# Projection of a filter-and-bilinear kernel: the third weight as the stationary operand, 512 tokens as the moving one

## The chip, the core and the metric

The kernel runs on one core of a Trainium2 chip. The metric is the device time of one execution in microseconds (us). The kernel before takes 2495.35 us, the median of three runs (2493.35 to 2497.64). Matmuls run on TensorE (PE in the profile; the load of a stationary operand is PEld), elementwise work on VectorE (DVE), ScalarE (ACT) and GpSimd (POOL); DMAs are issued from the SyncE (SP) and ScalarE queues.

## The reference

```
x: (8, 3072, 256)   filt_r, filt_i: (1537, 256)   w_a, w_b: (256, 1536)   w_out: (1536, 256)

X = np.fft.rfft(x, axis=1)
y = np.fft.irfft(X * (filt_r + 1j * filt_i)[None], n=3072, axis=1)   # a filter along the sequence
t = y.reshape(8 * 3072, 256)
out = ((t @ w_a) * (t @ w_b)) @ w_out                                # (24576, 256), fp32
```

The change touches only the last product, `(a * b) @ w_out`, and the order in which its result is stored.

## The kernel before, in words

**Tiling.** The transform along the sequence is made as matrix products of length 24 and 128 (the lines `s1`, `s2`, `is1`, `is2`, each on one pair of columns, row groups or token groups at a time). The rest works on visits `(b, c, p)`: batch `b` of 8, column group `c` of 6 (512 tokens each), slice `p` of 6 (256 of the 1536 hidden features). That is 288 visits. For a visit, seven products (`product`, the bilinear step with fewer multiplications) go to the PSUM banks x, y and z, ACT and DVE add them up to `c0` and `c1`, DVE multiplies their halves (`parts`, L678) to two gated tiles `g` of 128 features by 512 tokens each, called f0 and f1.

**Two halves of a number.** TensorE's fast fp32r form keeps fewer bits than fp32. So each operand is split in a high and a low half: `split` makes `gh` on ACT (L686) and then `gl = g - gh` on POOL (L687), and the third weight lies in SBUF as `wo_h` and `wo_l` for good. A product is three matmuls: high by high, low weight by high, high weight by low.

**The projection.** `project(r, f)` (L691) adds one gated tile, times its 128 rows of `w_out`, to the column group's result. That stands in two PSUM banks `po0` and `po1` over the 12 projections of a column group (6 slices by f0 and f1), 576 projections in all. Before, a block of 128 tokens of `gh` or `gl` is the stationary operand and the 256 columns of the weight move: 4 blocks by 3 terms is 12 matmuls of 256 columns. A result has tokens on partitions. All of them go through `mm` (L223), which reads the moving operand alternately from its first and its second half:

```
out, m = out.rearrange("p (a k) -> p a k", k=2), m.rearrange("p (k a) -> p a k", k=2)
nc.tensor.matmul(out, w, m, **kw)
```

With 256 moving columns the two halves are 128 numbers, 512 bytes, apart. The 512-column matmuls of `turn` (L441, L442) alternate at the same 512 bytes, once for each half of their columns. The start of the kernel has 512-column fp32r matmuls that are read straight on (`first_s1`, L524).

**What sets the order.** The order is written out by hand under a manual schedule. In each visit, PE does the products 1, 2, 5 and 6, then `project(one, 1)`, the f1 half of the visit before last; then the products 7 and 3, one step of the next batch's transform, `project(prev[-1], 0)`, the f0 half of the last visit, and product 4. `split` of f0 stands ahead of the projection by about half a visit, that of f1 by almost one. On POOL the `gl` subtractions stand in one queue with those of the transform (`xl` L393, `yl` L468) and of `is2` (`al` L656). In the first batch the weights are converted on the side.

**The end of a column group.** `store` (L708) has DVE copy `po0` and `po1` to one tile `ot`, and SP stores it; `keep` does so to SBUF for the first batch's first two column groups, whose slices come in two parts. The last column group ends in `store_last` (L718), with smaller pieces on two queues.

Of the kernel before, what the change touches and what calls it, by code (L numbers as in the profile page):

```python
# [9 lines left out]
F32 = mybir.dt.float32  # L10
# [8 lines left out]
B, S, D, DFF = 8, 3072, 256, 1536  # L19
N1, N2 = 128, 24  # L20
# [4 lines left out]
NC = 6  # L25
# [8 lines left out]
def _halves(order):  # L34

    return np.asarray(order).reshape(-1, 2).T.ravel()


FILTERED = _halves(range(D))
# [179 lines left out]
def fft_filter_bilinear_kernel(ctx: ExitStack, tc, x, x0, filt, fny, filt0, fny0, wa, wb, wo, s1c, gc, fc, fl, ic, sc, s1f, ff, fi, out):  # L219
    nc = tc.nc  # L220
    f32 = lambda t: t.bitcast(F32)

    def mm(out, w, m, **kw):  # L223

        out, m = out.rearrange("p (a k) -> p a k", k=2), m.rearrange("p (k a) -> p a k", k=2)
        nc.tensor.matmul(out, w, m, **kw)  # L226
# [12 lines left out]
    later, moe = [], []  # L239
# [31 lines left out]
    wo_h = [const.tile([128, 2, D], F32R, name=f"woh{p}") for p in range(NP)]  # L271
    wo_l = [const.tile([128, 2, D], F32R, name=f"wol{p}") for p in range(NP)]
# [82 lines left out]
    for k, p in ORDER:  # L355
        if k == "o":
            conv.append([wo.bitcast(I32).rearrange("(f p) (d w) -> p f d w", p=128, w=2)[:, 2 * p:2 * p + 2], p, 2])
        else:
            w = (wa if k == "a" else wb).bitcast(I32).rearrange("(k p) (f w) -> p k f w", p=128, w=2)
# [328 lines left out]

    po = {}

    def project(r, f, some=range(4)):  # L691
        b, c, p = r["at"]
        gh, gl = (t.rearrange("p h (n m) -> p (h n) m", n=2) for t in r[f"f{f}"])
        if p == r["from"] and f == 0:
            po[b, c] = [ps_o.tile([128, 2, D], F32, name=f"po{i}", tag=f"po{i}") for i in range(2)]
        for n in some:
            o = po[b, c][n // 2][:, n % 2]
            for q, (g, w) in enumerate(((gh, wo_h), (gh, wo_l), (gl, wo_h))):
                mm(
                    o, g[:, n], w[p][:, 1 - f], start=p == r["from"] and f == 0 and n % 2 == 0 and q == 0,  # L700
                    stop=p == r["to"] and f == 1 and q == 2, skip_group_check=True,
                )

    def keep(c):
        for i, t in enumerate(po.pop((0, c))):
# [2 lines left out]
    def store(b, c):  # L708
        ot = moe[0].tile([128, 4, D], F32, name="ot", tag="ot")
        for i, t in enumerate(po.pop((b, c))):  # L710
            if (b, c) in ((0, 0), (0, 1)):
                nc.vector.tensor_tensor(out=ot[:, 2 * i:2 * i + 2], in0=t, in1=filts[c][:, i], op=ALU.add)
            else:
                nc.vector.tensor_copy(out=ot[:, 2 * i:2 * i + 2], in_=t)
        nc.sync.dma_start(out=out[S * b:S * b + S].rearrange("(p n) d -> p n d", n=N2)[:, 4 * c:4 * c + 4], in_=ot)


    def store_last(b, c, i):  # L718
        ot, to = moe[0].tile([128, 2, D], F32, name="ol", tag=f"g{'f0' if i else 'f1'}"), out[S * b:S * b + S].rearrange("(p n) d -> p n d", n=N2)
        t = po[b, c][i]  # L720
        if i == 0:
            nc.vector.tensor_copy(out=ot, in_=t)
            nc.sync.dma_start(out=to[:, 4 * c:4 * c + 2], in_=ot)
            return
        nc.scalar.copy(out=ot[:, 0], in_=t[:, 0])
        nc.vector.tensor_copy(out=ot[:, 1], in_=t[:, 1])
        nc.scalar.dma_start(out=to[:, 4 * c + 2:4 * c + 3], in_=ot[:, 0:1])
        nc.sync.dma_start(out=to[:, 4 * c + 3:4 * c + 4], in_=ot[:, 1:2])


    STEPS = {
# [44 lines left out]
    with tc.manual_schedule():  # L776
# [90 lines left out]
        for b in range(B):  # L867
# [5 lines left out]
            o = 0 if b else 15  # L873
# [6 lines left out]
            if b + 1 < B:  # L880
# [4 lines left out]
                for i in range(NI):  # L885

                    t = o + i if b == 0 else 2 * i
# [6 lines left out]
                t = 28 if b else 30  # L894
# [4 lines left out]
                for i in range(NJ):  # L899
                    t = 30 + 2 * i if b else 32 + 2 * i  # L900
# [22 lines left out]
            for v, (c, p) in enumerate(VISITS if b == 0 else [(c, p) for c in range(NC) for p in range(NP)]):  # L923
# [3 lines left out]
                r = {"at": (b, c, p), "from": NP // 2 if halves and p >= NP // 2 else 0, "to": NP // 2 - 1 if halves and p < NP // 2 else NP - 1}  # L927
# [19 lines left out]
                if len(prev) == 2:  # L947
                    one = prev.pop(0)
                    project(one, 1)
                    if one["at"][2] == NP - 1:  # L950
                        store(*one["at"][:2])
                    elif one["at"][2] == one["to"]:
                        keep(one["at"][1])
# [9 lines left out]
                if prev:  # L963
                    project(prev[-1], 0)
# [9 lines left out]
        one, r = prev  # L974
        parts(r, r["c1"], "f1")
        split(r, "f1", nc.vector)
        project(one, 1)
        project(r, 0)
        for i in range(2):
            project(r, 1, range(2 * i, 2 * i + 2))  # L980
            store_last(*r["at"][:2], i)


# [37 lines left out]
```

## Time and profile before

| | before |
|---|---|
| median of 3 runs | 2495.35 us |
| the profiled execution's own time | 2497.37 us |
| its span in the profile | 2495.5 us |
| PE, PEld busy | 2448.1 us (98%), 2384.9 us (96%) |
| DVE, ACT, POOL busy | 1799.7 (72%), 1408.8 (56%), 1229.5 us (49%) |
| matmuls | 20934 |
| mean traffic of HBM | 125 GB/s |

The profile is one execution. Matmuls overlap in it: a 256-column matmul is listed with 275 ns although the next one starts after some 111 ns, so the busy time of PE isn't a count of work, and the distance from one start to the next is what a matmul costs in a stream. A line number can be that of a helper: all matmuls through `mm` stand under L226, and the names of the tiles tell them apart (`po<-woh,gh` is a matmul of the projection).

### The profile page before, as it was taken

The page shows a single profiled execution, that of the slowest core. Times are in us where ns is not written, and L with a number is a line of the kernel's source. Part 1 is how long each engine was busy: PE and PEld are TensorE (multiplying, and loading weights), DVE is VectorE, ACT ScalarE, POOL GpSimd, SP SyncE. Part 2 cuts the span into 40 slices and gives each one's busy share as a digit, 9 for nine tenths or more (in the row PEclk, how much of TensorE's full clock was granted, in tenths as well). Part 3 has the DMA queues.
Part 4 walks back from the last instruction along what each step waited for, and adds up shares of the span by engine and source line. Part 5 has one row for each costly group of instructions (what it writes and reads, how often), then busy time and mean ns, then how long its engine had stood idle before and what let it go on. Part 6 is the DMA issues. An engine that isn't in the chain of part 4 may idle for free.

```text
span 2495.5 us, 53409 instructions
## 1 busy us (share of the span) xinstructions
PE 2448.1 (98%) x20934; PEld 2384.9 (96%) x20934; DVE 1799.7 (72%) x2511; ACT 1408.8 (56%) x2480; POOL 1229.5 (49%) x926
## 2 busy tenths in 40 slices
PE   7889999999999999999999999999999999999999
PEld 3589999999999999999999999999999999999999
DVE  6875996569955798568975589656996569955555
ACT  5755555555556555565555555565555555555554
POOL 4765454545544554454545445454554545434333
PEclk9999999999999999999999999999999999999999
DMA  9437442444334453245523454145442544310100
GB/s 302 155 126 244 137 133 76 163 142 143 111 101 140 150 153 113 85 144 161 153 81 110 155 156 137 62 140 165 139 122 70 166 142 141 113 38 23 43 22 18
DMA packets 209423, 310.65 MB, mean 124 GB/s; under 512 B 19186, under 2 KB 119476, under 8 KB 209092
## 3 DMA queue, kind: packets, MB, share of 16 engines
q1 hardware_dynamic: 166580, 230.55, 30.0%
q10 hardware_dynamic: 42592, 76.70, 8.8%
q8 instruction: 164, 2.69, 0.4%
q14 instruction: 87, 0.71, 0.1%
HBM read 202.31 MB, written 108.45 MB: 125 GB/s over the span
## 4 chain that ended last, share of the span: by engine, by line
PE 83%; DVE 5%; POOL 4%; issue 4%; DMA 2%; ACT 2%; SPq 0%; ACTq 0%; DVEq 0%; POOLq 0%
PE po L226 27%; PE x L226 27%; PE z L226 13%; PE y L226 7%; PE ps L635 3%; PE ps L226 2%; POOL gl L687 1%; PE ps L442 1%; PE ps L441 1%; POOL al L656 1%; DVE g L678 1%; POOL yl L468 1%; DMA filt<-in_filt 1%; DVE c L937 1%; DVE v L454 1%
## 5 line engine op out<-in xcount | busy, mean ns | idle before, releaser
L687 POOL TENSOR_TENSOR gl<-g,gh 128x512 fp32r<-128x512 f32 x574 | 755.1, 1318 | 819.6 <-ACT gh L686 790.9
L678 DVE TENSOR_TENSOR g<-c 128x512 f32<-128x512 f32 x576 | 541.1, 939 | 277.4 <-ACT c L968 142.8
L226 PE MATMUL po<-woh,gh 128*128 128x256 f32 x2304 | 641.4, 278 | 0.7 <-DVE filt L706 0.7
L226 PE MATMUL po<-woh,gl 128*128 128x256 f32 x2304 | 635.9, 276 | 4.5 <-POOL gl L687 3.8
L226 PE MATMUL po<-wol,gh 128*128 128x256 f32 x2304 | 633.6, 275 | 0.0
L968 ACT COPY c<-x 128x512 f32<-128x512 f32 x288 | 169.0, 587 | 694.6 <-PE x L226 635.2
L226 PEld LDWEIGHTS po<-woh,gl 128*128 128x128 f32 x2304 | 442.2, 192 | 8.5 <-POOL gl L687 8.2
L226 PEld LDWEIGHTS po<-woh,gh 128*128 128x128 f32 x2304 | 442.3, 192 | 7.8 <-DVE filt L706 0.9
L226 PEld LDWEIGHTS po<-wol,gh 128*128 128x128 f32 x2304 | 442.3, 192 | 5.0
L686 ACT CAST gh<-g 128x512 fp32r<-128x512 f32 x576 | 357.6, 621 | 70.4 <-PE po L226 43.7
L226 PE MATMUL x<-ah,wah 128*128 128x256 f32 x1152 | 318.2, 276 | 9.3 <-ACT c L932 6.0
L226 PE MATMUL x<-al,wah 128*128 128x256 f32 x1152 | 317.0, 275 | 0.1
L226 PE MATMUL x<-ah,wal 128*128 128x256 f32 x1152 | 316.9, 275 | 0.0
L226 PE MATMUL x<-ah,wbh 128*128 128x256 f32 x1152 | 316.9, 275 | 0.0
L226 PE MATMUL x<-al,wbh 128*128 128x256 f32 x1152 | 316.9, 275 | 0.0
L226 PE MATMUL x<-ah,wbl 128*128 128x256 f32 x1152 | 316.9, 275 | 0.0
L957 DVE TENSOR_TENSOR c<-x,c 128x512 f32<-128x512 f32 x288 | 197.9, 687 | 163.9 <-PE x L226 161.4
L226 PEld LDWEIGHTS x<-ah,wah 128*128 128x128 f32 x1152 | 221.3, 192 | 11.6 <-ACT c L932 7.1
L226 PEld LDWEIGHTS x<-al,wah 128*128 128x128 f32 x1152 | 221.3, 192 | 0.3 <-DVE al L646 0.3
L226 PEld LDWEIGHTS x<-ah,wbh 128*128 128x128 f32 x1152 | 221.3, 192 | 0.0
L226 PEld LDWEIGHTS x<-al,wbh 128*128 128x128 f32 x1152 | 221.3, 192 | 0.0
L226 PEld LDWEIGHTS x<-ah,wbl 128*128 128x128 f32 x1152 | 221.3, 192 | 0.0
(145 smaller groups left out, 6002.9 us busy)
## 6 DMA issues: line engine op xcount, KB each, us to landing
z<-zh ACTq DMA_DIRECT2D x112, 256.0 KB, 2.3
filt<-in_filt SPq DMA_DIRECT2D x112, 256.0 KB, 2.8
zth<-z SPq DMA_DIRECT2D x112, 256.0 KB, 3.0
tt<-td SPq DMA_DIRECT2D x94, 256.0 KB, 4.3
out<-ot SPq DMA_DIRECT2D x47, 512.0 KB, 3.0
td<-t ACTq DMA_DIRECT2D x114, 192.0 KB, 2.1
xt<-in_x SPq DMA_DIRECT2D x84, 256.0 KB, 3.9
st<-s1d SPq DMA_DIRECT2D x84, 256.0 KB, 2.7
```

The costliest lines, as they stand in the source:

```text
L226: nc.tensor.matmul(out, w, m, **kw)
L441: nc.tensor.matmul(out, w[:, 0], hi, start=True, stop=False)
L442: nc.tensor.matmul(out, wl[:, 0], lo, start=False, stop=True)
L454: nc.vector.scalar_tensor_tensor(out=v[half[1 - a]], in0=ps[half[a]], scalar=sct[half[a], a:a + 1], in1=fm[half[1]], op0=ALU.mult, op1=ALU ...
L468: nc.gpsimd.tensor_tensor(out=yl, in0=y, in1=f32(yh), op=ALU.subtract)
L635: nc.tensor.matmul(to, tt[:, n, 128 * k:128 * k + 128], gt[:, n].rearrange("p (k a) -> p k a", k=2), start=True, stop=True)
L656: nc.gpsimd.tensor_tensor(out=al[:, 3 + i:5 + i], in0=t[:, i:i + 2], in1=f32(ah[:, 3 + i:5 + i]), op=ALU.subtract)
L678: nc.vector.tensor_tensor(out=gt, in0=g[:, :, 0], in1=g[:, :, 1], op=ALU.mult)
L686: nc.scalar.copy(out=gh, in_=gt)
L687: low.tensor_tensor(out=gl, in0=gt, in1=f32(gh), op=ALU.subtract)
L957: nc.vector.tensor_tensor(out=c1[:, 1], in0=bx, in1=c1[:, 1], op=ALU.add)
L968: nc.scalar.copy(out=c1[:, 0], in_=bx)
```

## The change

The operands of the projection change places. A block of 128 columns of the weight is stationary, and all 512 tokens of `gh` or `gl` move at once: 2 blocks by 3 terms is 6 matmuls of 512 columns. The result has the 256 columns of `w_out` on partitions (128 in each bank) and tokens along the free dimension. The accumulating matmuls of the two banks alternate, term by term (high by high into both banks, then the low weight, then the low tokens); only in the first and the last projection of a column group they stand bank by bank. `mm` now alternates between two halves of 256 tokens, 1024 bytes apart. The tile that is stored goes out as it stands, to an output of its own shape that is contiguous for a column group, and numpy on the host turns it to the reference's layout. The columns of `w_out` are given in their own order.

```diff
--- before.py
+++ after.py
@@ -688,18 +688,18 @@
 
     po = {}
 
-    def project(r, f, some=range(4)):
+    def project(r, f, some=range(2)):
         b, c, p = r["at"]
-        gh, gl = (t.rearrange("p h (n m) -> p (h n) m", n=2) for t in r[f"f{f}"])
+        gh, gl = (t.rearrange("p h m -> p (h m)") for t in r[f"f{f}"])
         if p == r["from"] and f == 0:
             po[b, c] = [ps_o.tile([128, 2, D], F32, name=f"po{i}", tag=f"po{i}") for i in range(2)]
-        for n in some:
-            o = po[b, c][n // 2][:, n % 2]
-            for q, (g, w) in enumerate(((gh, wo_h), (gh, wo_l), (gl, wo_h))):
-                mm(
-                    o, g[:, n], w[p][:, 1 - f], start=p == r["from"] and f == 0 and n % 2 == 0 and q == 0,
-                    stop=p == r["to"] and f == 1 and q == 2, skip_group_check=True,
-                )
+        begins, ends = p == r["from"] and f == 0, p == r["to"] and f == 1
+        passes = [(i, q, *w) for q, w in enumerate(((wo_h, gh), (wo_l, gh), (wo_h, gl))) for i in some]
+        for i, q, w, g in sorted(passes, key=lambda e: e[0]) if begins or ends else passes:
+            mm(
+                po[b, c][i].rearrange("p n d -> p (n d)"), w[p][:, 1 - f, 128 * i:128 * i + 128], g,
+                start=begins and q == 0, stop=ends and q == 2, skip_group_check=True,
+            )
 
     def keep(c):
         for i, t in enumerate(po.pop((0, c))):
@@ -712,20 +712,20 @@
                 nc.vector.tensor_tensor(out=ot[:, 2 * i:2 * i + 2], in0=t, in1=filts[c][:, i], op=ALU.add)
             else:
                 nc.vector.tensor_copy(out=ot[:, 2 * i:2 * i + 2], in_=t)
-        nc.sync.dma_start(out=out[S * b:S * b + S].rearrange("(p n) d -> p n d", n=N2)[:, 4 * c:4 * c + 4], in_=ot)
+        nc.sync.dma_start(out=out[b, c], in_=ot)
 
 
     def store_last(b, c, i):
-        ot, to = moe[0].tile([128, 2, D], F32, name="ol", tag=f"g{'f0' if i else 'f1'}"), out[S * b:S * b + S].rearrange("(p n) d -> p n d", n=N2)
+        ot, to = moe[0].tile([128, 2, D], F32, name="ol", tag=f"g{'f0' if i else 'f1'}"), out[b, c]
         t = po[b, c][i]
         if i == 0:
             nc.vector.tensor_copy(out=ot, in_=t)
-            nc.sync.dma_start(out=to[:, 4 * c:4 * c + 2], in_=ot)
+            nc.sync.dma_start(out=to[:, 0:2], in_=ot)
             return
         nc.scalar.copy(out=ot[:, 0], in_=t[:, 0])
         nc.vector.tensor_copy(out=ot[:, 1], in_=t[:, 1])
-        nc.scalar.dma_start(out=to[:, 4 * c + 2:4 * c + 3], in_=ot[:, 0:1])
-        nc.sync.dma_start(out=to[:, 4 * c + 3:4 * c + 4], in_=ot[:, 1:2])
+        nc.scalar.dma_start(out=to[:, 2:3], in_=ot[:, 0:1])
+        nc.sync.dma_start(out=to[:, 3:4], in_=ot[:, 1:2])
 
 
     STEPS = {
@@ -977,7 +977,7 @@
         project(one, 1)
         project(r, 0)
         for i in range(2):
-            project(r, 1, range(2 * i, 2 * i + 2))
+            project(r, 1, (i,))
             store_last(*r["at"][:2], i)
 
 
@@ -1004,7 +1004,7 @@
     arrays = {
         "x": given(np.asarray(x)[:, :, GIVEN]), "x0": given(x0),
         "filt": given(filt), "fny": given(fny), "filt0": given(filt0), "fny0": given(fny0),
-        "wa": given(moe_w_a), "wb": given(moe_w_b), "wo": given(np.asarray(moe_w_out)[:, FILTERED]),
+        "wa": given(moe_w_a), "wb": given(moe_w_b), "wo": given(np.asarray(moe_w_out)),
         "s1c": s1c, "gc": gc, "fc": fc, "fl": fl, "ic": ic,
         "sc": sc, "s1f": s1f, "ff": ff, "fi": fi,
     }
@@ -1013,8 +1013,9 @@
         nc.dram_tensor(f"in_{n}", a.shape, mybir.dt.from_np(a.dtype), kind="ExternalInput").ap()
         for n, a in arrays.items()
     ]
-    out = nc.dram_tensor("out", (B * S, D), F32, kind="ExternalOutput").ap()
+    out = nc.dram_tensor("out", (B, NC, 128, 4, D), F32, kind="ExternalOutput").ap()
     with tile.TileContext(nc) as tc:
         fft_filter_bilinear_kernel(tc, *args, out)
     r = _run(nc, [{f"in_{n}": a for n, a in arrays.items()}], core_ids=[0])
-    return r.results[0]["out"]
+    turned = r.results[0]["out"].reshape(B, NC, 128, 2, 2, N1, 2)
+    return np.ascontiguousarray(turned.transpose(0, 5, 1, 6, 4, 3, 2)).reshape(B * S, D)
```

PE's order, in a visit of slice 0: the f1 projection of the column group before, slice 4 (`woh_103` and `wol_109` are the two halves of its weight, `po_...` the two banks). Before:

```order
L226 MATMUL x<-ah,wbl_86 128x256
L226 MATMUL po_4525<-woh_103,gh 128x256
L226 MATMUL po_4525<-wol_109,gh 128x256
L226 MATMUL po_4525<-woh_103,gl 128x256 [waits Pool_49]
L226 MATMUL po_4525<-woh_103,gh 128x256
L226 MATMUL po_4525<-wol_109,gh 128x256
L226 MATMUL po_4525<-woh_103,gl 128x256
L226 MATMUL po_4526<-woh_103,gh 128x256
```

After:

```order
L226 MATMUL x<-ah,wbl_86 128x256
L226 MATMUL po_4165<-gh,woh_103 128x512
L226 MATMUL po_4166<-gh,woh_103 128x512
L226 MATMUL po_4165<-gh,wol_109 128x512
L226 MATMUL po_4166<-gh,wol_109 128x512
L226 MATMUL po_4165<-gl,woh_103 128x512 [waits Pool_49]
L226 MATMUL po_4166<-gl,woh_103 128x512
L226 MATMUL x<-ah,wah_83 128x256 [waits Activation_49]
```

Five more rows of the second bank follow before. The wait for POOL's `gl` stands at the third of 12 matmuls before, behind two of 256 columns; now it stands at the fifth of 6, behind four of 512 columns.

PE's order where a column group begins, its slice 0, f0 half; the waits for DVE are for the copy of the last result out of each bank. Before:

```order
L226 MATMUL po_4525<-woh_99,gh 128x256 [waits DVE_49]
L226 MATMUL po_4525<-wol_105,gh 128x256
L226 MATMUL po_4525<-woh_99,gl 128x256 [waits Pool_49]
L226 MATMUL po_4525<-woh_99,gh 128x256
L226 MATMUL po_4525<-wol_105,gh 128x256
L226 MATMUL po_4525<-woh_99,gl 128x256
L226 MATMUL po_4526<-woh_99,gh 128x256 [waits DVE_49]
L226 MATMUL po_4526<-wol_105,gh 128x256
```

After:

```order
L226 MATMUL po_4165<-gh,woh_99 128x512 [waits DVE_49]
L226 MATMUL po_4165<-gh,wol_105 128x512
L226 MATMUL po_4165<-gl,woh_99 128x512 [waits Pool_49]
L226 MATMUL po_4166<-gh,woh_99 128x512 [waits DVE_49]
L226 MATMUL po_4166<-gh,wol_105 128x512
L226 MATMUL po_4166<-gl,woh_99 128x512
L226 MATMUL x<-ah,wah_87 128x256 [waits DVE_49]
```

Here the banks stay apart: the wait for `gl` is at the third matmul in both, behind two of 256 columns before and two of 512 now, and each bank's wait for DVE is at its first matmul as it was. On POOL the order of instructions is the same, word for word; on DVE, ACT and SP it differs in buffer numbers alone.

## Rows read from the trace of the kernel before

**Rows 1.** The page, part 1: busy time of each engine, share, instructions.

```profile
PE 2448.1 (98%) x20934; PEld 2384.9 (96%) x20934; DVE 1799.7 (72%) x2511; ACT 1408.8 (56%) x2480; POOL 1229.5 (49%) x926
```

**Rows 2.** The page, part 4: the chain that ended last, shares of the span by engine.

```profile
PE 83%; DVE 5%; POOL 4%; issue 4%; DMA 2%; ACT 2%; SPq 0%; ACTq 0%; DVEq 0%; POOLq 0%
```

**Rows 3.** Stretches: engine, busy us and (instructions); PEclk is the granted clock.

```profile
core 0: us, PE busy (x) PEld busy (x) DVE busy (x) ACT busy (x) POOL busy (x), PEclk, DMA share, GB/s
1500.00:1600.00 100.00, 99.47 (x853) 97.80 (x852) 85.60 (x114) 56.23 (x101) 50.22 (x38) 1.00 0.39 120
2300.00:2400.00 100.00, 100.00 (x898) 100.00 (x898) 54.41 (x84) 52.15 (x92) 41.77 (x33) 1.00 0.09 28
```

**Rows 4.** The page, part 5: matmuls and weight loads of the projection.

```profile
L226 PE MATMUL po<-woh,gh 128*128 128x256 f32 x2304 | 641.4, 278 | 0.7 <-DVE filt L706 0.7
...
L226 PE MATMUL po<-woh,gl 128*128 128x256 f32 x2304 | 635.9, 276 | 4.5 <-POOL gl L687 3.8
...
L226 PEld LDWEIGHTS po<-woh,gl 128*128 128x128 f32 x2304 | 442.2, 192 | 8.5 <-POOL gl L687 8.2
```

**Rows 5.** Timeline, PE, 612.87 to 614.65 us: start us, us, engine line operation.

```profile
612.87 0.38 PE L441 MATMUL ps<-zth,fct 128*128 128x512 f32 x1
613.09 0.38 PE L442 MATMUL ps<-ztl,flt 96*128 96x512 f32 x1
613.31 0.28 PE L226 MATMUL po<-woh,gh 128*128 128x256 f32 x1
...
614.65 0.28 PE L226 MATMUL x<-ah,wah 128*128 128x256 f32 x1
```

**Rows 6.** Timeline, PE, the next projection, 618.00 to 620.31 us.

```profile
618.00 0.38 PE L441 MATMUL ps<-yh,ict 128*96 128x512 f32 x1
...
618.43 0.27 PE L226 MATMUL po<-woh,gh 128*128 128x256 f32 x1
618.54 0.28 PE L226 MATMUL po<-wol,gh 128*128 128x256 f32 x1
619.09 0.38 PE L226 MATMUL po<-woh,gl 128*128 128x256 f32 x1 [0.28 <-POOL gl L687]
619.30 0.28 PE L226 MATMUL po<-woh,gh 128*128 128x256 f32 x1
619.42 0.28 PE L226 MATMUL po<-wol,gh 128*128 128x256 f32 x1
...
620.31 0.28 PE L226 MATMUL x<-ah,wah 128*128 128x256 f32 x1
```

**Rows 7.** Waits of the weight loads (PEld): us in total, times, longest us.

```profile
PEld po L226 <- POOL gl L687: 8.2, 20, 0.5
```

**Rows 8.** Timeline, POOL, around the same projection.

```profile
613.03 3.07 POOL L656 TENSOR_TENSOR al<-t,ah 128x512 fp32r<-128x512 f32 x2 [3.52 <-ACT ah L655]
616.07 1.29 POOL L468 TENSOR_TENSOR yl<-y,yh 128x512 fp32r<-128x512 f32 x1
617.31 2.96 POOL L687 TENSOR_TENSOR gl<-g,gh 128x512 fp32r<-128x512 f32 x2
```

**Rows 9.** Timeline, PE, start of the kernel: 512 columns read straight on.

```profile
18.91 0.39 PE L524 MATMUL ps<-xl,sh 128*128 128x512 f32 x1
19.14 0.40 PE L524 MATMUL ps<-xh,sl 128*128 128x512 f32 x1
...
19.84 0.39 PE L524 MATMUL ps<-xh,sl 128*128 128x512 f32 x1
```

**Rows 10.** The same stretch of the start: DMA share and GB/s.

```profile
0.00:25.00 25.00, 15.22 (x38) 9.00 (x39) 11.31 (x20) 8.20 (x15) 10.70 (x12) 1.00 0.85 313
```

**Rows 11.** Waits of the matmuls (PE): the longest total among them.

```profile
PE x L226 <- ACT c L932: 6.0, 6, 1.5
```

**Rows 12.** The page, part 6: the store of a finished column group.

```profile
out<-ot SPq DMA_DIRECT2D x47, 512.0 KB, 3.0
```

## The prediction

> **What bounds the kernel now.** I read the busy shares first, then the chain of waits, then stretches of 100 us, and at last single projections on the timeline. PE is busy 98% of the span, DVE 72%, all others less [rows 1], and PE holds 83% of the chain that ended last [rows 2]. In the stretch from 2300 us, where no transform of a next batch runs, 898 matmuls and 898 weight loads stand in 100 us, at a granted clock of 1.00, the 2.4 GHz level: PE has no free time there, while DVE is busy 54.41 us [rows 3]. In the stretch from 1500 us, with the transform beside it, PE is busy 99.47 us, DVE 85.60. So the time is the sum of the distances between matmul starts, plus a few stalls. The listed durations (278 ns for a matmul, 192 ns for a load, 2304 of each kind [rows 4]) overlap; distances count.
>
> **What the change removes and adds on PE.** The columns that pass are the same: 12 matmuls of 256 are 3072, and 6 of 512 are 3072. What goes is half of the matmuls, so whatever each costs beyond its columns. At 2.4 GHz 256 columns take 106.7 ns and 512 take 213.3.
>
> One projection before: 12 matmuls from 613.31 to 614.65 us, 1.34 us, 111.7 ns each [rows 5]; the quiet stretch gives 100 us / 898 = 111.4 [rows 3]. So a matmul costs some 5 ns beyond its columns. For 512 columns the trace has the pairs L441 and L442: 612.87 to 613.31 and 618.00 to 618.43, four matmuls in 0.87 us, 217.5 ns each [rows 5, 6]: some 4 ns beyond the columns. The extra goes by the matmul, not by the column. Six such take 1.305 us, 0.035 us less than before. There are 576 projections (2304 matmuls of each kind over the 4 blocks [rows 4]): 576 x 0.035 = 20.2 us.
>
> [...]
>
> **How the new moving operand is read.** This is the term that no row shows. The 217.5 ns were measured with the operand read alternately from places 512 bytes apart. Now they are 1024 bytes apart, and nothing in the kernel before reads so. That the reading can matter is seen at the start of the kernel: matmuls of 512 columns in the same fp32r form, read straight on, start 0.93 us / 4 = 232.5 ns apart (18.91 to 19.84 us) [rows 9], 15 ns more than the alternating ones, though there the DMA engines were at 0.85 of their time [rows 10]. So the price of one new matmul lies between 217.5 and 232.5 ns; below 217.5 there are only the 4.2 ns down to the bare columns, 14 us over 3456 matmuls. I take 217.5, from the row that is nearest in kind: alternating, same width, same output of a whole bank, in the same stretches of the kernel.
>
> **Weight loads.** They fall from 12 to 6 in a projection. A load takes 192 ns [rows 4] and was hidden behind matmuls 111 ns apart; behind 217 ns it is hidden better, and L441 and L442 show that a 512-column matmul and the 256-column one behind it follow without a gap [rows 5]. The stationary operand is now a tile that lies ready in SBUF.
>
> **The stall on `gl`.** In some projections PE reaches the third matmul before POOL has made `gl`. At 618.54 the distance is 0.55 us (619.09) where 0.11 is due, and the next is 0.21 (619.30): 0.54 us lost [rows 6]. The weight loads show it 20 times, 8.2 us in all, at most 0.5 [rows 7]; with the 0.1 us behind each, 8.2 + 2.0 = 10.2 us. POOL is late because `is2` and the transform put work ahead: it runs from 613.03 without a gap through `al`, `yl` and two `gl` [rows 8]. These are f1 projections of slice 4, neither first nor last of their group, so their new order has four matmuls of 512 columns ahead of the wait for `gl`: 0.87 us, against 0.22 before. That is 0.65 us more slack, and the longest wait is 0.5. All of it should go: -10.2 us. What would be late next: the same `gl` by another 0.15 us, and then PE's other waits, of which the largest total is 6.0 us in 6 waits for ACT's `c` [rows 11]. The visits behind a stall now start half a microsecond earlier; their cover is that POOL and ACT are busy about half of the time [rows 1, 3].
>
> **What costs nothing, and its cover.** DVE's copies, `keep` and the store have the same shapes, and POOL's queue has the same order; each partition still writes 4 KB in one piece, and a store lands in 3.0 us [rows 12] with visits of some 8.3 us (2497 / 288 less the start) before `ot` is used again. If a store were late, it would hold up DVE, not PE. The new layout is made on the host. In the first batch PE also waits for others (the 6.0 us of ACT's `c` fall there); of the shorter projections ahead of about 300 us, some 40 of them, 1.4 us can be lost to such waits; I take 1.
>
> **The sum** against the profiled execution's own time: 2497.4 - 20.2 - 10.2 + 1 = 2468 us. That execution lies 2.0 us above the median of the runs, and 0.3 under the highest; against the median the same sum gives 2466. I say 2467.
>
> **Rivals.**
> A. *The 1024-byte alternation reads like straight reading.* 232.5 ns a matmul, 1.395 us a projection, +0.055 us, times 576 = +31.7 us; with the stall gone, 2497.4 + 31.7 - 10.2 = 2519 us, slower. For it: the pattern costs 15 ns where it differs [rows 9], and no row has the new distance. Against it: what the alternation seems to buy is that neighbouring columns come from different places, which 1024 bytes do as well, and the 15 ns may in part be the busy DMA [rows 10]. It decides from 1.34 + 10.2 / 576 = 1.358 us a projection on, 226 ns a matmul.
> B. *The stall stays or moves.* PE, with less in front of it, meets POOL or ACT elsewhere, and the 10.2 us come back at other places: 2477 us. For it: POOL's chain in such a visit is not shortened. Against it: it is late in one visit of six at most, and idle half of the time.
> C. *The extra of a matmul is smaller than the timeline's two digits say.* One distance of L441 reads 0.22 [rows 5]; at 220 ns a projection takes 1.32 us, the gain is 11.5 us, and the time 2476 us. [...]
> D. *The change doesn't do what it says*: a load of the new stationary operand isn't hidden where the wait for `gl` sits on the same matmul, so that the load starts when `gl` comes. That was so before too (the wait is listed at the load [rows 7]), and costs at most 0.1 us where a stall is left. It moves the forecast by 2 us and is inside its range.
>
> **Chances.** The forecast 0.68, its own range 2461 to 2474; B and C together 0.14; A 0.15; something faster still (a matmul nearer to its bare columns, down to 2454) 0.03. The range 2457 to 2487 holds the forecast, B and C, and leaves A out; 0.82 of the chance. A measurement of this kernel tells about 0.2%, 5 us, from no change: faster is 2490 or less, all of the forecast, B, C and a reading price up to 224 ns: 0.82. Within 0.2%, a price between 224 and 228 ns: 0.05. Slower, from 228 ns up: 0.13.
>
> **What the profile after would show.** PE has 3456 matmuls `po<-gh,woh` of 512 columns; two of them start 0.217 us apart (A: 0.23), six take 1.30 us. The wait of the projection for POOL's `gl` is gone from PE's list (B: another wait of some 8 us stands there). The quiet stretch from 2300 us, where there are no such stalls, holds fewer matmuls in the same time but the work of a visit takes 0.07 us less. DVE, ACT and POOL have the same instructions and durations. The prediction is wrong if the distance of the new matmuls is over 220 ns, or if the PE waits grow by more than 5 us anywhere after 300 us.

## The result, and the profile after

The changed kernel takes 2466.15 us, the median of four runs (2459.34 to 2468.24); the kernel before, beside it on the same chip, 2494.35. The ratio is 0.9882, with a 95% interval of 0.9858 to 0.9906. The forecast was 2467, with a range of 2457 to 2487. The profiled execution took 2464.96 us, its span is 2463.2, so 32.4 us less than the profiled one before.

The page's busy times and the chain that ended last, to compare with [rows 1, 2]:

```profile
PE 2420.0 (98%) x17478; PEld 2263.9 (92%) x17478; DVE 1780.7 (72%) x2511; ACT 1405.0 (57%) x2480; POOL 1223.0 (50%) x926
...
PE 93%; DMA 2%; issue 2%; ACT 1%; DVE 1%; POOL 1%; SPq 0%; ACTq 0%; POOLq 0%; DVEq 0%
```

PE now holds 93% of the chain, where it held 83%, and POOL 1% instead of 4%. The quiet stretch, 2250 to 2350 us here, as in [rows 3]; then the same stretch for the instructions on the tiles `po` alone:

```profile
core 0: us, PE busy (x) PEld busy (x) DVE busy (x) ACT busy (x) POOL busy (x), PEclk, DMA share, GB/s
2250.00:2350.00 100.00, 100.00 (x752) 95.83 (x752) 54.38 (x83) 52.26 (x91) 39.19 (x30) 1.00 0.08 27
```

```profile
2250.00:2350.00 100.00, 38.30 (x156) 27.55 (x156) 2.68 (x4) 0.00 (x0) 1.00 0.08 27
```

752 matmuls stand in 100 us, 156 of them of the projection. The other 596, at the 111.4 ns of before, take 66.4 us, which leaves 33.6 us for 156: 215.4 ns each. One projection on the timeline, the f1 half of slice 4 of the same column group as in [rows 6] (start us, us; `x2` are two matmuls in a row):

```profile
611.30 0.38 PE L441 MATMUL ps<-yh,ict 128*96 128x512 f32 x1
611.51 0.38 PE L442 MATMUL ps<-yl,ict 128*96 128x512 f32 x1
611.73 0.59 PE L226 MATMUL po<-gh,woh 128*128 128x512 f32 x2
612.16 0.59 PE L226 MATMUL po<-gh,wol 128*128 128x512 f32 x2
612.59 0.59 PE L226 MATMUL po<-gl,woh 128*128 128x512 f32 x2
613.02 0.27 PE L226 MATMUL x<-ah,wah 128*128 128x256 f32 x1
```

Six matmuls take 1.29 us (611.73 to 613.02), where twelve took 1.34 [rows 5]. The start times of all neighbouring matmuls of the projection in the trace, stalls left out, lie 216.2 ns apart on average; it was 111.6. And the wait for `gl` that stood here before is not there, although POOL is no earlier:

```profile
606.42 3.06 POOL L656 TENSOR_TENSOR al<-t,ah 128x512 fp32r<-128x512 f32 x2 [3.52 <-ACT ah L655]
609.44 1.28 POOL L468 TENSOR_TENSOR yl<-y,yh 128x512 fp32r<-128x512 f32 x1
610.68 2.97 POOL L687 TENSOR_TENSOR gl<-g,gh 128x512 fp32r<-128x512 f32 x2
```

POOL's two `gl` run from 610.68 to 613.65; the first ends at 612.42 in the trace, 0.69 us after the projection's start. The projection asks for it 0.86 us after its start, at 612.59. Between 300 and 2400 us PE's list of waits has one row left, which was there before too:

```profile
PE ps L635 <- DMA gt<-in_gc: 1.6, 1, 1.6
```

The rows of the projection's matmuls and loads, as in [rows 4]; there are 1152 matmuls of each of the three kinds, 3456 in all (the prediction gave all 3456 to `po<-gh,woh`). No row of the matmuls names POOL any more. The loads' engine is idle for longer before them (32.6 us here), since six loads now lie beside the columns that twelve lay beside:

```profile
L226 PE MATMUL po<-gh,woh 128*128 128x512 f32 x1152 | 369.5, 388 | 2.6 <-DVE filt L706 2.6
...
L226 PE MATMUL po<-gl,woh 128*128 128x512 f32 x1152 | 359.8, 380 | 0.0
...
L226 PEld LDWEIGHTS po<-gl,woh 128*128 128x128 f32 x1152 | 217.3, 189 | 32.6 <-DVE gl L687 0.4
```

### The profile page after: what moved, and what is told of

Read it like the earlier page. It is cut to its first block, busy times and chain, and to the rows that moved or that the text cites. A ratio compares the mean times of both kernels' runs of the same rounds, so it can differ in the third digit from the quotient of the medians.

```text
span 2463.2 us, 46508 instructions
## 1 busy us (share of the span) xinstructions
PE 2420.0 (98%) x17478; PEld 2263.9 (92%) x17478; DVE 1780.7 (72%) x2511; ACT 1405.0 (57%) x2480; POOL 1223.0 (50%) x926
## 4 chain that ended last, share of the span: by engine, by line
PE 93%; DMA 2%; issue 2%; ACT 1%; DVE 1%; POOL 1%; SPq 0%; ACTq 0%; POOLq 0%; DVEq 0%
PE x L226 30%; PE po L226 30%; PE z L226 15%; PE y L226 7%; PE ps L635 3%; PE ps L226 3%; PE ps L441 2%; PE ps L442 2%; DMA filt<-in_filt 1%; PE ps L556 0%; POOL xl L393 0%; PE ps L524 0%; DMA zf<-z 0%; DVE g L678 0%; DMA gt<-in_gc 0%
## 5 line engine op out<-in xcount | busy, mean ns | idle before, releaser
L687 POOL TENSOR_TENSOR gl<-g,gh 128x512 fp32r<-128x512 f32 x574 | 745.1, 1301 | 788.8 <-ACT gh L686 762.5
L678 DVE TENSOR_TENSOR g<-c 128x512 f32<-128x512 f32 x576 | 509.1, 884 | 271.1 <-ACT c L968 134.0
L226 PE MATMUL po<-gh,woh 128*128 128x512 f32 x1152 | 369.5, 388 | 2.6 <-DVE filt L706 2.6
L226 PE MATMUL po<-gl,woh 128*128 128x512 f32 x1152 | 359.8, 380 | 0.0
L226 PE MATMUL po<-gh,wol 128*128 128x512 f32 x1152 | 359.8, 380 | 0.0
L226 PEld LDWEIGHTS po<-gl,woh 128*128 128x128 f32 x1152 | 217.3, 189 | 32.6 <-DVE gl L687 0.4
L226 PEld LDWEIGHTS po<-gh,wol 128*128 128x128 f32 x1152 | 218.3, 190 | 29.3
L656 POOL TENSOR_TENSOR al<-t,ah 128x512 fp32r<-128x512 f32 x96 | 146.3, 1544 | 152.3 <-ACT ah L655 152.3
L226 PEld LDWEIGHTS x<-ah,wal 128*128 128x128 f32 x1152 | 221.3, 192 | 0.0
```

The lines of the kernel that those rows point to most:

```text
L656: nc.gpsimd.tensor_tensor(out=al[:, 3 + i:5 + i], in0=t[:, i:i + 2], in1=f32(ah[:, 3 + i:5 + i]), op=ALU.subtract)
L678: nc.vector.tensor_tensor(out=gt, in0=g[:, :, 0], in1=g[:, :, 1], op=ALU.mult)
L687: low.tensor_tensor(out=gl, in0=gt, in1=f32(gh), op=ALU.subtract)
```

## The experiments

All times are medians; a ratio is to the kernel before, measured beside it (its median was 2497.89 us beside the first, second, third and sixth experiment, 2498.47 beside the others), with its 95% interval. In the code, `...` stands for lines left out.

**Bank by bank: the wait moved forward.**

```diff
-        for i, q, w, g in sorted(passes, key=lambda e: e[0]) if begins or ends else passes:
+        for i, q, w, g in sorted(passes, key=lambda e: e[0]):
```

> The changed kernel, but every projection goes bank by bank (three terms into po0, then three into po1), so the wait for gl stands behind two matmuls of 512 columns (0.43 us) and not behind four. Theory (the wait for gl was hidden by the order): POOL's gl comes 0.57 to 0.69 us after the projection's start in 21 projections, so 0.14 to 0.26 us of wait come back in each, with some 0.1 us behind it: about 6 us, 2472 us. Rival (the stall went because of the wider matmuls alone, the order has no part in it): the time of the changed kernel, 2466 us, and no wait for POOL's gl.

Measured: 2471.69 us, ratio 0.9893 (0.9881 to 0.9906). The same projection on the timeline, and the weight loads' wait for `gl` between 300 and 2400 us (us, times, longest):

```profile
614.86 0.38 PE L226 MATMUL po<-gh,woh 128*128 128x512 f32 x1
615.08 0.38 PE L226 MATMUL po<-gh,wol 128*128 128x512 f32 x1
615.61 0.48 PE L226 MATMUL po<-gl,woh 128*128 128x512 f32 x1
615.92 0.38 PE L226 MATMUL po<-gh,woh 128*128 128x512 f32 x1
```

```profile
PEld po L226 <- POOL gl L687: 10.3, 20, 0.6
```

The third matmul starts 0.53 us after the second (0.22 are due), the fourth 0.31 after it: 0.40 us lost here, in one of 20 waits. The stall is back at its old place, so it is the order that hides it. By the distances of the third and the fourth matmul the 20 waits cost 7.6 us together, where 6 were expected. The time by itself doesn't separate this kernel from the changed one, since the intervals overlap; the rows do.

**The kernel before, with `gl` last.**

```diff
-        for n in some:
-            o = po[b, c][n // 2][:, n % 2]
-            for q, (g, w) in enumerate(((gh, wo_h), (gh, wo_l), (gl, wo_h))):
...
+        passes = [(n, q) for q in range(3) for n in some]
+        for n, q in sorted(passes, key=lambda e: (e[0] // 2, e[1] == 2)) if begins or ends else passes:
+            g, w = ((gh, wo_h), (gh, wo_l), (gl, wo_h))[q]
...
```

> The kernel before (tokens stationary, 256 columns moving, 12 matmuls) with only the order changed: the eight matmuls with gh first, the four with gl last (bank by bank in the first and last projection of a column group). Theory (two separate gains, one from the width and one from the place of the gl wait): the stall on gl goes, 10 us under the kernel before, 2484 us; distances stay at 111.7 ns. Rival (the whole gain is the width's; the stall would come back elsewhere in this order): within 3 us of the kernel before, 2494 us, with another wait of 8 us on PE.

Measured: 2489.69 us, ratio 0.9966 (0.9954 to 0.9977), 8 us under the kernel before (6 to 11 by the interval). A projection of slice 4, f1, on the timeline:

```profile
611.16 0.61 PE L226 MATMUL po<-woh,gh 128*128 128x256 f32 x4
611.61 0.61 PE L226 MATMUL po<-wol,gh 128*128 128x256 f32 x4
612.05 0.61 PE L226 MATMUL po<-woh,gl 128*128 128x256 f32 x4
612.50 0.28 PE L226 MATMUL x<-ah,wah 128*128 128x256 f32 x1
```

Twelve matmuls in 1.34 us, as before, and no wait for `gl` in the list from 300 to 2400 us. So the order alone gives some 8 us, without the exchange of operands; the whole change gave 28.

**Weight stationary, but 256 tokens at a time.**

```diff
-            mm(
-                po[b, c][i].rearrange("p n d -> p (n d)"), w[p][:, 1 - f, 128 * i:128 * i + 128], g,
-                start=begins and q == 0, stop=ends and q == 2, skip_group_check=True,
-            )
+            for h in range(2):
+                mm(
+                    po[b, c][i][:, h], w[p][:, 1 - f, 128 * i:128 * i + 128], g[:, 256 * h:256 * h + 256],
+                    start=begins and q == 0 and h == 0, stop=ends and q == 2, skip_group_check=True,
+                )
```

The host's layout is turned to fit.

> The changed kernel with each matmul of 512 tokens cut in two of 256 (12 matmuls again; the weight stays stationary and is loaded for each; order of the terms as in the changed kernel; alternation at 512 bytes). Theory (the gain of the width is a cost per matmul): distances of 111.7 ns, 576 x 0.043 us = 25 us given back, the gl wait still gone: 2484 to 2491 us, the same as the kernel before with gl last. Rival (the gain comes from the exchange of operands, the weight that lies ready being the stationary one, and not from the width): 2466 us.

Measured: 2490.63 us, ratio 0.9963 (0.9951 to 0.9975): the same as the kernel before with `gl` last, within the intervals. Eleven of the twelve matmuls:

```profile
1001.65 0.61 PE L226 MATMUL po<-gh,woh 128*128 128x256 f32 x4
1002.09 0.61 PE L226 MATMUL po<-gh,wol 128*128 128x256 f32 x4
1002.54 0.50 PE L226 MATMUL po<-gl,woh 128*128 128x256 f32 x3
```

Four take 0.44 to 0.45 us, and there is no wait for `gl` from 300 to 2400 us. So at 256 columns it makes no difference which operand is stationary. The gain needs the 512 columns; with them goes the number of loads, 6 or 12, and no run here changes one without the other.

**The same 256, read from places 1024 bytes apart.**

```diff
-            mm(
-                po[b, c][i].rearrange("p n d -> p (n d)"), w[p][:, 1 - f, 128 * i:128 * i + 128], g,
...
+            for n in range(2):
+                nc.tensor.matmul(
+                    po[b, c][i][:, n].rearrange("p (a k) -> p a k", k=2), w[p][:, 1 - f, 128 * i:128 * i + 128],
+                    g.rearrange("p (k m) -> p m k", k=2)[:, 128 * n:128 * n + 128],
...
```

> Twelve matmuls of 256 columns with the weight stationary, as in the experiment before with 256, but with alternation at 1024 bytes. Theory (the cost is the matmul's, whatever the distance): 111.7 ns, 2490 us. Rival (the 512-byte distance costs part of the 5 ns that a 256-column matmul takes beyond its columns): 110 ns or less, 2484 us or less; then the bilinear products would gain from it too.

Measured: 2489.1 us, ratio 0.9963 (0.9952 to 0.9974); the mean distance is 111.6 ns, at 1024 bytes as at 512. So the bilinear products, which also have 256 columns at 512 bytes, should have nothing to gain from 1024; that was not run.

**512 tokens, read from places 512 bytes apart.**

```diff
-            mm(
-                po[b, c][i].rearrange("p n d -> p (n d)"), w[p][:, 1 - f, 128 * i:128 * i + 128], g,
+            nc.tensor.matmul(
+                po[b, c][i].rearrange("p n (a k) -> p n a k", k=2), w[p][:, 1 - f, 128 * i:128 * i + 128],
+                g.rearrange("p (j k a) -> p j a k", j=2, k=2),
```

The host's layout is turned to fit.

> The changed kernel (512 moving columns, 6 matmuls) with alternation at 512 bytes, as the transform's 512-column matmuls have it, in place of 1024. Theory (the distance between the two halves does not matter, only that there are two): distances of 216 to 218 ns, 2466 to 2472 us. Rival (each kind of reading has its own price, and 1024 bytes is a better one): distances of 220 ns or more, 2480 us.

Measured: 2465.33 us, ratio 0.9866 (0.985 to 0.9883), and on the timeline 0.43 to 0.44 us for two:

```profile
1000.48 0.60 PE L699 MATMUL po<-gh,woh 128*128 128x512 f32 x2
1000.92 0.59 PE L699 MATMUL po<-gh,wol 128*128 128x512 f32 x2
1001.35 0.59 PE L699 MATMUL po<-gl,woh 128*128 128x512 f32 x2
```

So 512 or 1024 bytes between the two places makes no difference at either width.

**512 tokens read straight on.** The matmul without the rearrangement of `mm`, the host's layout turned to fit.

```diff
-            mm(
-                po[b, c][i].rearrange("p n d -> p (n d)"), w[p][:, 1 - f, 128 * i:128 * i + 128], g,
+            nc.tensor.matmul(
+                po[b, c][i].rearrange("p n d -> p (n d)"), w[p][:, 1 - f, 128 * i:128 * i + 128], g,
```

> The changed kernel with the 512 moving tokens read straight on instead of alternately from two halves (the host's layout is changed to fit). Theory (alternation buys some 15 ns per 512 columns, at 1024 bytes as at 512): distances of 232 ns in place of 216, 3456 x 16 ns = 55 us, 2521 us. Rival (the 232 ns seen at the start of the kernel came from the busy DMA engines there): distances of 216 ns and 2466 us.

Measured: 2522.27 us, ratio 1.0092 (1.0078 to 1.0107). Slower than before, and near the 2519 us that rival A of the prediction gave for this price. Two matmuls take 0.47 us:

```profile
1003.65 0.64 PE L699 MATMUL po<-gh,woh 128*128 128x512 f32 x2
1004.12 0.62 PE L699 MATMUL po<-gh,wol 128*128 128x512 f32 x2
```

Over all pairs it is 234.0 ns. The 232.5 ns of the kernel's start [rows 9] were the reading's own price, not that of the busy DMA engines: in this run's stretch from 2250 to 2350 us, where these stand at 0.12 of their time, the distance is 233 ns (median of 126 pairs).

**512 tokens read from four places in turn.**

```diff
-            mm(
-                po[b, c][i].rearrange("p n d -> p (n d)"), w[p][:, 1 - f, 128 * i:128 * i + 128], g,
+            nc.tensor.matmul(
+                po[b, c][i].rearrange("p n (a k) -> p (n a) k", k=4), w[p][:, 1 - f, 128 * i:128 * i + 128],
+                g.rearrange("p (k a) -> p a k", k=4),
```

The host's layout is turned to fit.

> The changed kernel with the 512 tokens read in turn from four places, 512 bytes apart, in place of two, 1024 apart. Theory (two places already hide what straight reading costs, the rest is the matmul's): 216 ns, 2466 us. Rival (more places hide more): towards the bare columns, 213.3 ns, 2456 us. Other side: four places are too many, 230 ns or more, 2515 us.

Measured: 2672.82 us, ratio 1.0697 (1.0679 to 1.0716). Two matmuls take 0.55 us:

```profile
1001.99 0.72 PE L699 MATMUL po<-gh,woh 128*128 128x512 f32 x2
1002.54 0.72 PE L699 MATMUL po<-gh,wol 128*128 128x512 f32 x2
1003.09 0.72 PE L699 MATMUL po<-gl,woh 128*128 128x512 f32 x2
```

Over all pairs 278.5 ns. Theory and first rival both fell; the third case, "230 ns or more, 2515 us", was right in sign and far too small in time: four places cost 62 ns more than two, where 230 ns would have been 14 more. One place costs 234 ns, two 216, four 278. The runs do not show why.

## Why the prediction was right

**The width.** Forecast 0.035 us a projection from two digits of the timeline; measured 12 x 111.6 - 6 x 216.2 = 42 ns, times 576 = 24 us where 20.2 were forecast. If a column is counted as the prediction counts it, as one cycle of 2.4 GHz, the 512-column matmul costs 2.9 ns beyond its columns, less than the 4 ns that the rows of L441 and L442 gave, and the 256-column one 5. (In a stretch at the 1.2 GHz level, shown in the last section, a 512-column matmul takes 427 ns, 0.83 ns a column: one cycle there too.) Counted so, the cost beyond the columns isn't one fixed sum per matmul, as the step said; it fell to less than half per projection (12 x 5 = 60 ns to 6 x 2.9 = 17). The mechanism was right, the term was 4 us too small. That the exchange of operands gives nothing by itself is shown by the experiments with 256 tokens: same stationary weight, and the gain of the width gone. Whether the 7 ns for each pair belong to the second matmul or to the second load stays open, since both went together.

**The reading.** The term that no row of before showed was taken at 217.5 ns, from the nearest kind, with the straight 232.5 as the other end. Both ends were right in what they stood for: alternating 216.2, straight 234.0. The price is that of alternating between two places, not of their distance.

**The stall.** Forecast -10.2 us by more slack at the wait for `gl`. The wait is gone, and it comes back where the order puts it forward again. In the kernel before, the 19 waits between 300 and 2400 us cost 9.1 us by the distances of the third and the fourth matmul, so the size was right too. POOL's `gl` comes 0.7 us behind the projection's start where it came 0.6 behind; the reserve of 0.15 us that the prediction named was enough.

**The sum.** With the measured width and the forecast stall it is 24 + 10 = 34 us; the profiled executions differ by 32.4 and the medians by 28.2 (interval of the ratio: 23 to 35 us). Where the kernel runs evenly it comes out: from the first `z` product of visit 25 (at 314.27 us before, 312.32 after) to that of visit 283 (2444.31 and 2411.19) the time is 31.2 us shorter, and the 516 projections between them account for 21.7 of it at 42 ns each, which leaves 9.5 for the stalls. The forecast lost 1 us at the start of the kernel and nothing at its end. The trace has three pieces that cost: a wait of 2 us for a copy of DVE and a second stretch at the lower clock, which cost about 1.4 us (both in the last section), and the end, 5.7 us from the last matmul's start to the span's end where it was 4.0. That end is ACT's issue of a last piece of the result, before and after:

```profile
2492.27 0.39 ACTq L727 DMA_DIRECT2D out<-ol  x1
```

```profile
2458.69 2.13 ACTq L727 DMA_DIRECT2D out<-ol  x1
```

Bank by bank, with the same store as the changed kernel, it took 0.39 us again, and in the kernel before with `gl` last, which has the old store, 1.90; so the new layout isn't what costs here, and the cause stays open. Other waits of the first batch became shorter, such as that for ACT's `c`, 4.5 us for 6.0 [rows 11], so that net the trace lost less than these three pieces:

```profile
PE x L226 <- ACT c L932: 4.5, 6, 1.4
...
PE po L226 <- DVE filt L706: 2.6, 2, 1.9
```

That the median fell within 1 us of the forecast is in part luck: the width gave 4 us more than forecast and the start and the end took some of it back, and the four runs lie between 2459 and 2468 us.

**The rivals.** A exists as a price (the straight reading) and does not apply to 1024 bytes. B did not come: after 300 us PE has no new wait but six of some 0.2 us, 1.3 us in all, for DVE's copy where a column group begins. C was off to the other side. D left nothing to see, since between 300 and 2400 us there is no stall left at `gl`.

The experiments point to no version clearly under the changed one: with the places 512 bytes apart it is the same within the intervals.

## What to carry to other kernels

Where PE is full, read the distance between matmul starts, not the listed durations, and count what a matmul costs beyond its columns: exchanging operands so that 512 columns move instead of 256 paid 7 ns for each pair replaced; the exchange paid nothing by itself. Put the matmuls whose operand comes last at the end of their group, over both banks; that alone was worth some 8 us, where the whole change gave 28, and needs no new layout. Before a new access pattern is put on the critical path, look for the nearest row in the trace, and price the other end too: of four ways to read the same 512 numbers two were equal, one was 18 ns slower and one 62.

## What the runs showed of the hardware

**Reading order.** For the same 512 fp32r columns: 216.2 ns from two places in turn, 234.0 straight on, 278.5 from four. The Trainium skill (SBUF — State Buffer, section Specifications (TRN2)) says that a 16-byte line needs at least two hits for full bandwidth and that each cross to a new line pays a penalty. By that, straight reading, four numbers to a line, should be the fastest of the three, and two and four places, which change the line with every number, should cost the same. The trace does not agree: two places are 18 ns faster than straight reading, and only four are slower.

**A DVE instruction held up by POOL.** The wait of 2 us, which ends at 136.5 us, comes from one instruction of the weight conversion, ahead of DVE's copy out of the bank. DVE's rows of the changed kernel, POOL's, and DVE's of the kernel before:

```profile
133.64 2.25 DVE L299 TENSOR_SCALAR t<-raw 128x512 int32<-128x512 int32 x1
135.81 1.28 DVE L706 COPY filt<-po 128x512 f32<-128x512 f32 x2
```

```profile
133.52 2.08 POOL L351 TENSOR_TENSOR wal<-m,wah 128x896 fp32r<-128x896 f32 x1 [0.70 <-ACT wah L350]
```

```profile
134.83 0.47 DVE L299 TENSOR_SCALAR t<-raw 128x512 int32<-128x512 int32 x1
135.20 1.30 DVE L706 COPY filt<-po 128x512 f32<-128x512 f32 x2
```

L299 took 2.25 us when it started 0.12 us behind POOL's L351, and ended 0.3 us after that did; before, where POOL's L351 began 0.05 us behind it (at 134.88 us), it took 0.47. The Trainium skill (SBUF — State Buffer, section Who interferes with whom) states that a `tensor_scalar` can run in a mode that takes ports which DVE shares with GpSimd, and that whichever issues first keeps them for its whole instruction while the other blocks; these rows agree, though no row shows the mode. All nine traces show the same two instructions at this place of the conversion. In the six where POOL's L351 began first, by 0.12 to 0.43 us, L299 took 1.95 to 2.25 us; in the three where L299 began first, by 0.05 to 0.12 us, it took 0.45 to 0.47 and L351 2.31 to 2.39 in place of some 2.09. So which of the two starts first decides on some 1.6 us here, and PE waits for it. It isn't a cost of the exchange: the kernel before with `gl` last is one of the six, and 256 tokens at 512 bytes is one of the three.

**The lower clock.** After two waits PE ran at half rate, over a whole projection:

```profile
228.19 0.28 PE L226 MATMUL z<-ah,wbl 128*128 128x256 f32 x1
229.88 0.38 PE L226 MATMUL ps<-xh,st 128*128 128x256 f32 x1 [1.41 <-ACT xh L392]
231.22 0.38 PE L226 MATMUL ps<-xl,st 128*128 128x256 f32 x1 [0.97 <-POOL xl L393]
...
232.25 1.06 PE L226 MATMUL po<-gh,woh 128*128 128x512 f32 x2
233.10 1.06 PE L226 MATMUL po<-gh,wol 128*128 128x512 f32 x2
233.96 1.06 PE L226 MATMUL po<-gl,woh 128*128 128x512 f32 x2
234.81 0.32 PE L226 MATMUL x<-ah,wah 128*128 128x256 f32 x1
```

```profile
232.00:235.50 3.50, 3.50 (x15) 2.96 (x14) 1.64 (x2) 0.58 (x1) 0.39 (x1) 0.59 0.16 61
```

The projection at 232.25 takes 2.56 us in place of 1.29: 427 ns a matmul, twice 216, the 1.2 GHz level; the granted clock is 0.59 on average over these 3.5 us, which costs 3.5 x 0.41 = 1.4 us. Ahead of it PE had waited 1.41 and 0.97 us within 3 us. Such stretches fall into the first 300 us of every trace, one to three in each between 30 and 240 us, and may be part of why runs of one kernel differ by a few microseconds; that was not tried.
